# Splitting the remainder rows of a feed-forward's weights in two parts, and moving a set's sums on GpSimd

## The chip, the cores and the metric

The kernel runs on one core of one Trainium2 chip. The core has five engines that follow their own instruction lists and meet at semaphores: TensorE (PE, its weight loads PEld), VectorE (DVE), ScalarE (ACT), GpSimd (POOL) and SyncE (SP), which issues most of the DMAs. The metric is the device time of one execution in microseconds. Before the change it is 1981.64 us, the median of three runs (1973.98 to 1981.75).

## The reference

One transformer block on 2048 tokens of width 576, all in float32. The attention part (32 heads of 18, in four segments of 512 tokens with a memory) ends some 655 us into the execution and is not touched. What follows is the feed-forward part:

```
h = layernorm(x) * (1 + cb) + sb
x = x + gb * ((silu(h @ w_gate) * (h @ w_up)) @ w_down)
```

w_gate and w_up are 576 x 4608, w_down is 4608 x 576, and gb scales the 576 columns of the result.

## The kernel before

**Seven products in place of eight.** The kernel takes the product of h with a pair of 128-column blocks of w_gate (or w_up), cut in 2 x 2, with a Strassen-like scheme (Winograd's): seven products m = 1 to 7 of sums and differences of blocks. The seven weight operands of one set stand in the seven slots of a tile O. Slots 0, 1 and 2 (m = 1, 2, 4) come from memory as they are: the plain weights. Slots 4, 5, 3 and 6 (m = 5, 6, 7, 3) are sums that GpSimd makes of blocks in O, by `sum_o(p, z, j)` with j = 0 to 3 in that order (L1089).

**Two words per number.** TensorE reads float32 rounded to a shorter form, so each weight is split: `prep_w` casts a slot to wh on ScalarE (L1098), and VectorE subtracts wh from it to get wl (L1099). A product (`prod`, L1134) is seven matmuls of 512 columns. Six of them use wh and wl on 2 x 128 rows of the contraction. The seventh uses wr, the 32 remainder rows of the 288, which stand three times over in 96 partitions. The wr tile of a set holds all seven slots, 7 x 128 = 896 columns; `prep_r` casts it at once (L1083) and subtracts partitions 32 to 63 (L1084).

**Loops.** There are two halves, t = 0 and 1 of 1024 tokens, and in each 18 pairs p of column blocks. A pair has two sets, z = 0 (gate) and z = 1 (up), so 14 steps k, one product each: z = 0 in steps 0 to 6, z = 1 in 7 to 13, in the order m = 1, 3, 6, 2, 7, 5, 4. The product m = 3 is that of the other set, one set late: step 1 uses set 1 of the pair before, and step 8 uses set 0. In the first half steps 4 to 11 also multiply a chunk of the pair before by the down weights (`plain`, L1254, twelve matmuls of 288 columns into pd), and VectorE adds it to acc (L1258).

**Banks.** The products of a set add up in three PSUM banks, A, B and C, and partial results are copied out on the way. After m = 1 ScalarE copies A to B (the B copy, L1179). After m = 6 it copies A to tb, after m = 7 to tc (L1162). VectorE adds C and tb after m = 3 (in set 1 into cu, L1156) and C and tc after m = 5. The next product into a bank waits until what stands in it has been copied.

**What sets the order.** It is written out by hand: what a step emits stands in each engine's list in the order of the code, and each engine goes through its list in order. VectorE's subtractions are put in `later` and emitted at the start of the next step. `prep_w` runs five products ahead (PF = 5), in the order MP. For the first half, before the change:

- Step 1 loads the pair's down weights into RW (`load_d`, L1106, SP), once RW is free of the wd store of the pair before. GpSimd scales them by gb at steps 4 and 5 (`mul_d`, L1112) and makes their four differences for the second half at 6 to 9 (`sum_d`, L1117). `prep_d` splits the four plain blocks (L1123, L1124) at steps 5, 6, 7 and 10.
- Step 2 loads set 0 of the next pair into O (`load_o`, L1069, SP), step 9 loads set 1. O has two buffers, one per set, and a load waits until the last readers of the buffer are done.
- GpSimd makes set 0's sums at steps 6 to 8. Of set 1's it makes two at 10 and 11, the other two at 4 and 5 of the next pair, each in front of a `mul_d`.
- `prep_r` of set 1 stands at step 6, that of the next set 0 at 9 (at 8 ahead of the second half).
- ScalarE's queue stores to memory what the second half reads again: the sums (`store_o`, oD, L1075), the rows (`store_r`, rD, L1092) and the down weights (wd, L1436). The second half loads them in place of making them (L1072, L1080, L1108).
- From the second pair on, steps 2 to 11 each advance a generator by one (`prep2`, `next(g2)`). It prepares the second half's h in small pieces on all engines, with DMAs of its own on SP (xl and xh rows, xb, yD).

Of the kernel before, what the change touches and what calls it, by code (L numbers as in the profile page):

```python
# [8 lines left out]
F32R = mybir.dt.float32r  # L9
BF16 = mybir.dt.bfloat16  # L10
AF = mybir.ActivationFunctionType
ALU = mybir.AluOpType
# [3 lines left out]
P = 128  # L16
# [18 lines left out]
PF = 5  # L35
# [34 lines left out]
def f32(ap):  # L70
    return ap.bitcast(F32)
# [3 lines left out]
def block(ctx: ExitStack, tc: tile.TileContext, x, wqk, wv, wo, beta, wgu, wd, c, w_mod, out):  # L75
    nc = tc.nc
# [76 lines left out]
    rD = [[dr.tile([96, 7, P], F32, tag=f"rD{p}_{z}", name=f"rD{p}_{z}") for z in range(2)] for p in range(NF // 2)]  # L153
# [93 lines left out]
    with ExitStack() as p1:  # L247
# [78 lines left out]
        with ExitStack() as p0:  # L326
# [27 lines left out]
            for p in (1, 0):  # L354
                for k in range(6):
                    for h in range(2):
                        r = 64 * (1 - p) + 32 * h
# [534 lines left out]

    p4 = ExitStack()
    NPR = NF // 2
    MP = (1, 6, 2, 7, 5, 4, 3)
    ZM = [(z if m != 3 else 1 - z, m) for z in range(2) for m in (1, 3, 6, 2, 7, 5, 4)]
    SLOT = {1: 0, 2: 1, 3: 6, 4: 2, 5: 4, 6: 5, 7: 3}
    ACT_OP = {1: 0, 2: 1, 3: 2, 4: 6, 5: 3, 6: 4, 7: 5}
# [175 lines left out]
    def store_o(p, z):  # L1074
        nc.scalar.dma_start(oD[p][z], O[p, z][:, 3:7, 0:2])  # L1075

    def prep_r(t, p, z):
        R[z] = r = wrp.tile([P, 7, P], F32R, tag="wr", name="wr")
        if t == 1:
            nc.sync.dma_start(f32(r[0:96]), rD[p][z])  # L1080
            return
        o = O[p, z]
        nc.scalar.copy(r[0:96], o[0:96, :, 2, :])  # L1083
        later.append(lambda: nc.vector.tensor_tensor(r[32:64], o[32:64, :, 2, :], f32(r[32:64]), op=ALU.subtract))  # L1084

    def sum_o(p, z, j):
        o = O[p, z]
        d, a, b, op = ((4, 3, 2, ALU.add), (5, 4, 0, ALU.subtract), (3, 0, 3, ALU.subtract), (6, 1, 5, ALU.subtract))[j]
        nc.gpsimd.tensor_tensor(o[:, d], o[:, a], o[:, b], op=op)  # L1089
# [20 lines left out]
    def mul_d(p, f):  # L1110
        v = RW[p][:, 2 * f:2 * f + 2].rearrange("p a b -> p (a b)")
        nc.gpsimd.tensor_tensor(v, v, gbB, op=ALU.mult)  # L1112

    def sum_d(p, j):
        r = RW[p]
        d, a, b = ((4, 1, 0), (5, 3, 4), (6, 2, 5), (1, 3, 1))[j]
        nc.gpsimd.tensor_tensor(r[:, d], r[:, a], r[:, b], op=ALU.subtract)  # L1117
# [155 lines left out]
    with tc.manual_schedule():  # L1273
# [51 lines left out]
        for i in range(4):  # L1325
            for h in range(2):
                for c in range(WC):
                    n = 8 * i + 4 * h + c
                    wo_m(3, i, h, c, 2)
                    if n in TT:  # L1330
                        next(gt, None)
                    if c == 3:
                        wo_x(3, i, h)
                    if n in EE:
                        next(ge, None)
                    if n in SS:
                        j = SS.index(n)
                        sum_o(0, j // 4, j % 4)
                    if n == WW[0]:
                        prep_r(0, 0, 0)  # L1340
                    if n in WW:
                        prep_w(0, 0, next(gw))
                        flush()
                if h == 1 and i < 2:
                    wo_r(3, i + 2)
                    wo_s(3, i + 2)
                    wo_t(3, i + 2)
# [26 lines left out]
        for t in range(2):  # L1374
            for p in range(NPR):
                last = t == 1 and p == NPR - 1
                nx = (p + 1) % NPR
                tn = t if nx else t + 1
                if t == 0 and p == NPR - 1:
                    run(g2)  # L1380
                    p6.close()
                    accq = pool(p4, "acq")
                    new_acc(accq, (1, 6, 7))
                if last:
                    load_x11(1)
                chunk = 0
                for k in range(14):
                    z, m = ZM[k]
                    todo, later[:] = later[:], []
                    while nw < len(seq) and nw <= n + PF:  # L1390
                        prep_w(*seq[nw])
                        nw += 1
                    n += 1
                    for f in todo:
                        f()
                    if k != 1 or prev is not None:
                        step(z, m)
                    if k == 1 and prev is not None:
                        PA[0, 1] = AC[0, 1]
                    if t == 0 and p == NPR - 1 and k in (7, 9, 10, 11, 12, 13) or t == 1 and p == 0 and k == 1:  # L1400
                        load_y(ACT_OP[m])
                    swap = t == 1 and p == 0
                    if not last and k == 7 - PF + swap:
                        load_o(tn, nx, 0)
                    elif not last and k == 14 - PF:
                        load_o(tn, nx, 1)
                    if k == (2 if t else 6):
                        prep_r(t, p, 1)
                    elif not last and k == (8 if t == 0 and tn else 9):
                        prep_r(tn, nx, 0)  # L1410
                    if t == 0:
                        if k == 1:
                            load_d(0, p)
                        elif k == 4 or k == 5:
                            if p:
                                sum_o(p, 1, k - 2)
                            mul_d(p, k - 4)
                        elif 6 <= k < 10 and p < NPR - 2:
                            sum_d(p, k - 6)
                        if tn == 0:  # L1420
                            if 5 < k < 9:
                                sum_o(nx, 0, k - 6)
                            if k == 8:
                                sum_o(nx, 0, 3)
                            elif k in (10, 11):
                                sum_o(nx, 1, k - 10)
                        if k == 0 and p == 0:
                            store_o(p, 0)
                        elif k == 3:
                            store_r(p, 0)  # L1430
                        elif k == 7:
                            store_o(p, 1)
                        elif k == 9:
                            store_r(p, 1)
                        elif k == 11:
                            nc.scalar.dma_start(wdD[p][:, :NS[p]], RW[p][:, :NS[p]])  # L1436
                        elif k == 12 and tn == 0:
                            store_o(nx, 0)
                    elif k == 2 + 2 * swap:
                        load_d(1, p)  # L1440
                    if prev is not None and is_plain(*prev):
                        if k in (0, 2):
                            ij = (1, 0) if k == 0 else (0, 1)
                            prep_a(prev[1] % 2, ij, PA[ij])
                        if CH0[t][k]:
                            f = plain(*prev, chunk)
                            if f:
                                late[k + 3] = f
                            chunk += 1
                        due(k)  # L1450
                    elif prev is not None:
                        for j in range(4):
                            if k == KS[j]:
                                sum_a(j)
                        if k == 0:
                            prep_a(prev[1] % 2, 2, PA[1, 0])
                        for j, kk in KA:
                            if k == kk:
                                prep_a(prev[1] % 2, j, PA[ASRC[j]])
                        for _ in range(CH[k]):  # L1460
                            down(*prev, chunk)
                            chunk += 1
                    if last and 1 <= k < 9:
                        comb(k - 1)
                    if p == 0 and (t, k) in RS:
                        load_res(t, RS[t, k])
                    if is_plain(t, p):
                        if k in (5, 6, 7, 10):
                            j = (5, 6, 7, 10).index(k)
                            prep_d(p, (j // 2, j % 2), j)  # L1470
                    elif k >= 7:
                        prep_d(p, POS[k - 7], WSLOT[POS[k - 7]])
                    for ij, kk, j in (((0, 0), 11, 1), ((1, 1), 13, 4)):
                        if k == kk:
                            prep_a(p % 2, ij if is_plain(t, p) else j, AC[ij])
                    if t == 0 and k in G2 and p > 0:
                        next(g2, None)
                for k in sorted(late):
                    due(k)
                PA.clear()  # L1480
                PA.update(AC)
                prev = (t, p)
# [61 lines left out]
```

## Time and profile before

| | |
|---|---|
| median of the runs | 1981.64 us |
| the profiled execution's own time | 1983.39 us |
| its span, first to last instruction | 1981.7 us |
| mean granted TensorE clock | 0.986 |
| first half of the feed-forward | 658 to 1338 us |
| second half | 1338 us to the end |
| PE waiting for wr of L1084, 672 to 1333 us | 39.1 us, 18 times |
| GpSimd waiting for O's load, same stretch | 132.5 us, 17 times |

The page gives each engine's busy time. A matmul's end is modelled, and matmuls overlap, so idle time in front of a matmul counts from the modelled end of the one before. In the list of waits a line has who waited, for whom, the sum in us, how often, and the longest. In the timeline a line has the start, the duration, engine, line of the code, operation, output<-inputs, shape, and in brackets the idle time of the engine in front of it and what ended that. In a table of stretches a line has the stretch, its length, the busy time of PE, PEld, DVE, ACT and POOL with the instructions of each, the granted clock, the share of DMA time and GB/s. An engine's idle time only counts where the engine is the bound or holds it up.

### The profile page before, as it was taken

How to read it: one execution, taken by the hardware profiler on the slowest of the kernel's cores; microseconds unless marked ns; L12 is line 12 of the kernel's file. 1: busy time of each engine (PE TensorE's matmuls, PEld its weight loads, DVE VectorE, ACT ScalarE, POOL GpSimd, SP SyncE). 2: the span in 40 equal slices, each digit the busy share in tenths (PEclk: the TensorE clock that was granted, in tenths of full speed). 3: DMA queues.
4: the chain of work that ended last, by engine and by line, in shares of the span. 5: the costliest groups of instructions: out<-in, count | busy, mean ns of one | idle time of the engine just before them, and what ended most of it. 6: DMA issues, size and time to landing. Idle time of an engine off the chain costs nothing.

```text
span 1981.7 us, 30522 instructions
## 1 busy us (share of the span) xinstructions
PE 1893.4 (96%) x10927; PEld 1574.8 (79%) x10927; DVE 1500.3 (76%) x3231; ACT 924.9 (47%) x2000; POOL 580.3 (29%) x772
## 2 busy tenths in 40 slices
PE   7999989999998899999999999999999999999999
PEld 4888856676776677888888887888888888888888
DVE  6575258878786877777777777765888888888887
ACT  2222267767666533444444443443454544454442
POOL 5212235555535544444344444420000000000000
PEclk9999999999999899999999999999999999999999
DMA  7767564545435644444454454449433333232331
GB/s 220 234 225 248 208 189 121 144 134 152 133 109 146 198 151 146 159 155 149 159 171 145 143 161 133 137 145 312 151 98 113 104 97 117 85 113 95 119 102 67
DMA packets 173543, 296.63 MB, mean 150 GB/s; under 512 B 25104, under 2 KB 101776, under 8 KB 171920
## 3 DMA queue, kind: packets, MB, share of 16 engines
q1 hardware_dynamic: 143392, 237.43, 38.8%
q10 hardware_dynamic: 30000, 57.25, 8.1%
q8 instruction: 86, 1.41, 0.3%
q14 instruction: 65, 0.53, 0.1%
HBM read 185.29 MB, written 109.31 MB: 149 GB/s over the span
## 4 chain that ended last, share of the span: by engine, by line
PE 86%; DVE 6%; DMA 5%; issue 1%; ACT 1%; POOL 1%; SPq 1%; ACTq 0%; DVEq 0%; POOLq 0%
PE A L1134 21%; PE pd L1254 12%; PE C L1134 12%; PE pd L1237 9%; PE B L1134 6%; PE pp L101 4%; PE s L589 4%; PE av L609 4%; PE s L187 4%; PE pv L101 3%; PE pw L707 2%; DVE wr L1084 1%; DVE wl L1099 1%; DMA mD<-mr 1%; PE pn L778 1%
## 5 line engine op out<-in xcount | busy, mean ns | idle before, releaser
L1134 PE MATMUL A<-y,wh 128*128 128x512 f32 x1152 | 406.6, 393 | 1.8 <-ACT tb L1162 0.9
L192 DVE CUSTOM_DVE_ANT_0 junk<-s,tri 128x256 bf16<-128x256 f32 (+3 forms) x512 | 228.9, 487 | 77.9 <-PE s L187 70.3
L1099 DVE TENSOR_TENSOR wl<-O,wh 128x256 fp32r<-128x256 f32 x504 | 259.7, 518 | 3.0 <-ACT wh L1098 2.5
L1134 PEld LDWEIGHTS A<-y,wh 128*128 128x128 f32 x1152 | 217.3, 189 | 46.0 <-ACT tb L1162 1.7
L1089 POOL TENSOR_TENSOR O<-O 128x384 f32<-128x384 f32 x144 | 166.5, 1165 | 229.0 <-DMA O<-in_wgu_dram 132.5
L1258 DVE TENSOR_TENSOR acc<-acc,pd 128x576 f32<-128x576 f32 x156 | 117.4, 753 | 151.4 <-PE pd L1254 151.3
L592 ACT ACTIVATE Pt<-s 128x512 f32<-128x512 f32 (+1 forms) x352 | 186.6, 558 | 88.5 <-PE s L589 73.7
L1134 PE MATMUL A<-y,wl 128*128 128x512 f32 x576 | 227.1, 394 | 0.0
L1134 PE MATMUL C<-y,wh 128*128 128x512 f32 x576 | 206.5, 399 | 0.0
L1242 DVE TENSOR_TENSOR acc<-acc,pd 128x576 f32<-128x576 f32 x216 | 162.1, 751 | 55.5 <-PE pd L1237 48.0
L1098 ACT CAST wh<-O 128x256 fp32r<-128x256 f32 x504 | 197.6, 404 | 0.1
L1254 PE MATMUL pd<-dh,al 128*128 128x288 f32 x640 | 192.5, 301 | 0.0
L1254 PE MATMUL pd<-dh,ah 128*128 128x288 f32 x640 | 192.2, 300 | 0.0
L1254 PE MATMUL pd<-dl,ah 128*128 128x288 f32 x640 | 192.0, 300 | 0.0
L589 PE MATMUL s<-qs,ks 110*128 110x512 f32 (+2 forms) x384 | 151.3, 411 | 5.5 <-DMA qs<-mD 3.9
L1198 DVE TENSOR_TENSOR al<-sg,ah 128x512 fp32r<-128x512 f32 x192 | 146.3, 762 | 13.6 <-ACT ah L1197 13.4
L1197 ACT CAST ah<-sg 128x512 fp32r<-128x512 f32 x192 | 118.6, 618 | 79.7 <-DVE sg L1157 79.5
L1134 PE MATMUL A<-y,wr 96*128 96x512 f32 x288 | 117.2, 407 | 40.4 <-DVE wr L1084 39.1
L187 PE MATMUL s<-ks,qs 108*128 108x256 f32 (+3 forms) x512 | 142.3, 329 | 3.0 <-DMA ks<-kD 1.2
L1149 ACT ACTIVATE sg<-sg 128x512 f32<-128x512 f32 x73 | 46.2, 633 | 196.6 <-DVE sg L1148 196.6
L1237 PE MATMUL pd<-dh,ah 128*128 128x288 f32 x448 | 133.0, 297 | 0.0
L1237 PE MATMUL pd<-dh,al 128*128 128x288 f32 x448 | 132.5, 296 | 0.0
(349 smaller groups left out, 4470.8 us busy)
## 6 DMA issues: line engine op xcount, KB each, us to landing
O<-in_wgu_dram SPq DMA_DIRECT2D x36, 768.0 KB
oD<-O ACTq DMA_DIRECT2D x36, 512.0 KB
O<-oD SPq DMA_DIRECT2D x36, 512.0 KB
ks<-kD SPq DMA_DIRECT2D x68, 216.0 KB
qs<-qD SPq DMA_DIRECT2D x68, 216.0 KB
O<-in_wgu_dram SPq DMA_DIRECT2D x36, 384.0 KB
rD<-wr ACTq DMA_DIRECT2D x36, 336.0 KB
wr<-rD SPq DMA_DIRECT2D x36, 336.0 KB
```

The costliest lines, as they stand in the source:

```text
L187: nc.tensor.matmul(bank[:, n * (h - h0):n * (h - h0) + n], lhsT=qst[b][0:108, h, 128 * i:128 * i + 128], rhs=kst[b][0:108, h // 2, 0:n], s ...
L192: nc.vector.tensor_tensor_reduce(junk[:, :n], bank[:, n * (h - h0):n * (h - h0) + n], tri[:, L - n:], 1.0, -3e38, op0=ALU.add, op1=ALU.max ...
L589: nc.tensor.matmul(bank[:, n * (g - h):n * (g - h + w)].rearrange("p (a b) -> p a b", a=w), lhsT=kst[u % NB][0:110, g // 2, 128 * j:128 * ...
L592: nc.scalar.activation(pt[:, h:h + per, :n], bank[:, :n * per].rearrange("p (a b) -> p a b", a=per), AF.Exp, scale=SCALE)
L1089: nc.gpsimd.tensor_tensor(o[:, d], o[:, a], o[:, b], op=op)
L1098: nc.scalar.copy(wh, o)
L1099: later.append(lambda: nc.vector.tensor_tensor(wl, o, f32(wh), op=ALU.subtract))
L1134: nc.tensor.matmul(bank, lhsT=a, rhs=b, start=(first and n == 0), stop=(n == 6), skip_group_check=not first)
L1198: later.append(lambda: nc.vector.tensor_tensor(al, src, f32(ah), op=ALU.subtract))
L1237: nc.tensor.matmul(pd[:, i, :288], lhsT=a[:, tk], rhs=w, start=(k == 0), stop=(k == 2))
L1242: nc.vector.tensor_tensor(o, o, pd[:, :, :288], op=ALU.add)
L1254: nc.tensor.matmul(pd[:, i, :288], lhsT=a[:, tk], rhs=w, start=(k == 0), stop=(k == 5))
```

## The change

- `prep_r` takes a part: part 0 is slots 0 to 2 (the plain weights, 384 columns), part 1 slots 3 to 6 (the sums, 512 columns), each with its own cast and subtraction. In the first half set 1's parts stand at steps 3 and 7, the next set 0's at 9 and 10.
- All four of set 1's sums move to steps 2 to 4 of the pair that uses them, in front of `mul_d`, which moves to 5 and 6. Set 0's sums move to 7 to 9, the differences of the down weights to 6, 7, 9 and 10.
- In the first half set 1 is loaded at step 12 in place of 9.
- m = 2 is split ahead of m = 6 (MP), and the casts of the down weights move to 6, 7, 8 and 10.
- The stores move: oD of set 1 from step 7 to 6, rD of set 1 from 9 to 10, wd from 11 to 12, oD of the next set 0 from 12 to 13.
- The second half's first load of set 1's rows goes to ScalarE's queue, at step 3 in place of 2.

```diff
-    MP = (1, 6, 2, 7, 5, 4, 3)
+    MP = (1, 2, 6, 7, 5, 4, 3)
...
-    def prep_r(t, p, z):
-        R[z] = r = wrp.tile([P, 7, P], F32R, tag="wr", name="wr")
+    def prep_r(t, p, z, part=0):
+        if part == 0:
+            R[z] = wrp.tile([P, 7, P], F32R, tag="wr", name="wr")
+        r = R[z]
         if t == 1:
-            nc.sync.dma_start(f32(r[0:96]), rD[p][z])
+            (nc.sync if p or z == 0 else nc.scalar).dma_start(f32(r[0:96]), rD[p][z])
             return
-        o = O[p, z]
-        nc.scalar.copy(r[0:96], o[0:96, :, 2, :])
-        later.append(lambda: nc.vector.tensor_tensor(r[32:64], o[32:64, :, 2, :], f32(r[32:64]), op=ALU.subtract))
+        o, c = O[p, z], slice(0, 3) if part == 0 else slice(3, 7)
+        nc.scalar.copy(r[0:96, c], o[0:96, c, 2, :])
+        later.append(lambda: nc.vector.tensor_tensor(r[32:64, c], o[32:64, c, 2, :], f32(r[32:64, c]), op=ALU.subtract))
...
                         prep_r(0, 0, 0)
+                        prep_r(0, 0, 0, 1)
...
-                    elif not last and k == 14 - PF:
+                    elif not last and k == (14 - PF if tn else 12):
                         load_o(tn, nx, 1)
-                    if k == (2 if t else 6):
-                        prep_r(t, p, 1)
-                    elif not last and k == (8 if t == 0 and tn else 9):
-                        prep_r(tn, nx, 0)
-                    if t == 0:
+                    if t:
+                        if k == 2 + swap:
+                            prep_r(1, p, 1)
+                        elif not last and k == 9:
+                            prep_r(1, nx, 0)
+                    else:
+                        if k in (3, 7):
+                            prep_r(0, p, 1, k // 7)
+                        elif tn == 0 and k in (9, 10):
+                            prep_r(0, nx, 0, k - 9)
+                        elif tn and k == 8:
+                            prep_r(1, 0, 0)
                         if k == 1:
                             load_d(0, p)
-                        elif k == 4 or k == 5:
-                            if p:
-                                sum_o(p, 1, k - 2)
-                            mul_d(p, k - 4)
-                        elif 6 <= k < 10 and p < NPR - 2:
-                            sum_d(p, k - 6)
-                        if tn == 0:
-                            if 5 < k < 9:
-                                sum_o(nx, 0, k - 6)
-                            if k == 8:
-                                sum_o(nx, 0, 3)
-                            elif k in (10, 11):
-                                sum_o(nx, 1, k - 10)
+                        elif k in (2, 3, 4) and p:
+                            for j in ((0, 1), (2,), (3,))[k - 2]:
+                                sum_o(p, 1, j)
+                        elif k in (5, 6):
+                            mul_d(p, k - 5)
+                        if tn == 0 and k in (7, 8, 9):
+                            for j in ((0,), (1, 2), (3,))[k - 7]:
+                                sum_o(nx, 0, j)
+                        if k in (6, 7, 9, 10) and p < NPR - 2:
+                            sum_d(p, (6, 7, 9, 10).index(k))
...
-                        elif k == 7:
+                        elif k == 6:
                             store_o(p, 1)
-                        elif k == 9:
+                        elif k == 10:
                             store_r(p, 1)
-                        elif k == 11:
+                        elif k == 12:
                             nc.scalar.dma_start(wdD[p][:, :NS[p]], RW[p][:, :NS[p]])
-                        elif k == 12 and tn == 0:
+                        elif k == 13 and tn == 0:
                             store_o(nx, 0)
-                    elif k == 2 + 2 * swap:
+                    if t and k == 2 + 2 * swap:
                         load_d(1, p)
...
-                        if k in (5, 6, 7, 10):
-                            j = (5, 6, 7, 10).index(k)
+                        if k in (6, 7, 8, 10):
+                            j = (6, 7, 8, 10).index(k)
                             prep_d(p, (j // 2, j % 2), j)
```

## The prediction, made before the result was known

> **What bounds the kernel now.** I read the page first (engine shares, then the slices), then the stretches of the two halves, the waits inside the first half, and the timeline around the largest of them.
>
> ```profile
> span 1981.7 us, 30522 instructions
> PE 1893.4 (96%) x10927; PEld 1574.8 (79%) x10927; DVE 1500.3 (76%) x3231; ACT 924.9 (47%) x2000; POOL 580.3 (29%) x772
> ...
> 658.00:1338.00 680.00, 638.22 (x3387) 555.12 (x3386) 517.09 (x765) 295.89 (x656) 295.28 (x265) 0.98 0.48 156
> 1338.00:1982.00 644.00, 638.15 (x3459) 559.60 (x3457) 532.12 (x970) 290.50 (x676) 0.00 (x0) 1.00 0.38 121
> ```
>
> TensorE is the bound. The last two lines are the two halves of the feed-forward (length, then busy time of PE, PEld, DVE, ACT and POOL, the granted clock, DMA). The second half leaves PE 5.9 us unbusy, the first, which the change edits, 41.8, and there the clock is 0.98 and not 1.00. What PE lacks stands in the waits between 672 and 1333 us:
>
> ```profile
> PEld A L1134 <- DVE wr L1084: 46.8, 18, 3.6
> PE A L1134 <- DVE wr L1084: 39.1, 18, 3.2
> ...
> ACT tb L1162 <- DVE cu L1156: 20.3, 10, 3.0
> ```
>
> One wait per pair, 18 in all, for the subtraction that ends the rows' split. The timeline shows why (start, duration, engine; in brackets the idle time in front):
>
> ```profile
> 899.75 0.93 ACT L1083 CAST wr<-O 96x896 fp32r<-96x896 f32 x1
> ...
> 900.86 0.75 DVE L1258 TENSOR_TENSOR acc<-acc,pd 128x576 f32<-128x576 f32 x1 [0.74 <-PE pd L1254]
> ...
> 901.53 0.52 DVE L1099 TENSOR_TENSOR wl<-O,wh 128x256 fp32r<-128x256 f32 x1
> ...
> 902.09 1.76 DVE L1084 TENSOR_TENSOR wr<-O,wr 32x896 fp32r<-32x896 f32 x1
> ...
> 903.91 0.51 PE L1134 MATMUL A<-y,wr 96*128 96x512 f32 x1 [1.70 <-DVE wr L1084]
> ```
>
> The rows are cast at step 6 and subtracted at the start of step 7. On VectorE the subtraction stands behind the accumulation of step 6's chunk, which can't begin before PE ends that chunk. From there VectorE needs 0.75 + 0.52 + 1.76 = 3.0 us, while PE has only six matmuls, 1.4 us, before step 7's seventh asks for the rows.
>
> **What the wait is worth.** The row's 39.1 us count from the modelled end of a matmul (0.39 us after its start), while starts that nothing holds are 0.23 apart: 0.16 more each, so 39.1 + 18 x 0.16 = 42.0 us. Some waits also cost clock. After the one at 744.79 (2.93 us) the matmuls stand 0.43 apart, and the 288-wide ones 0.24 and not 0.13:
>
> ```profile
> 747.42 0.63 PE L1134 MATMUL C<-y,wh 128*128 128x512 f32 x1
> 747.85 0.63 PE L1134 MATMUL C<-y,wl 128*128 128x512 f32 x1
> ```
>
> Six at +0.11 and four at +0.20 make 1.5 us. Of stretches cut one to a pair, seven or eight show such a clock (0.95 to 0.97): 7.5 x 1.5 = 11 us; bounds 0 and, from the mean clock of 0.98 over 666 us, 13.3.
>
> **The change part by part.** Steps are numbered as in the loop: 0 to 3, 12 and 13 take PE 1.62 us each, 4 to 11, with a chunk, 3.2.
>
> Rows in two parts. Set 1's plain part (384 of 896 columns) is cast at step 3 and subtracted at 4, three steps before its use at 7; the sums' part is cast at 7, subtracted at 8, used at 9. For that one the distance from the end of step 7's chunk to the use is 1.62 + 1.6 + 1.4 = 4.6 us, and VectorE needs 0.75 (accumulate) + 1.65 (the slow wl at 965.82, beside GpSimd) + 1.1 for 512 columns slowed as the 896 above (1.76 for 1.08) = 3.5. The wait goes: -42.0 and -11; what is late next, the sums' part, has 1.1 us of cover. Set 0's parts (steps 9, 10) precede uses at 0 and 2 by three steps or more.
>
> More instructions: 37 more casts and subtractions. From 256 columns at 0.42 and 896 at 1.08 a subtraction has a fixed 0.16, 6 us on VectorE in all; a cast (0.40, 0.93) a fixed 0.19, 7 us on ScalarE. They hide in VectorE's 128.4 us of waiting for pd (110 times) and ScalarE's idle half: 0, bound +6.
>
> Set 1's sums. Before, two stood at steps 10 and 11, where GpSimd waited for the load (132.5 us in 17 waits, off the path), and two among the multiplications. Now all four run as soon as the load lands, ahead of mul_d, and so fall near steps 12 to 4, where VectorE is densest. That stretch now, in the pair from 959.95 on:
>
> ```profile
> 962.48 1.43 POOL L1112 TENSOR_TENSOR dr__11702<-dr__11702,gbB 128x576 f32<-128x576 f32 x1 [4.89 <-DMA dr__11702<-in_wd_dram]
> ...
> 962.91 1.56 DVE L1198 TENSOR_TENSOR al<-sg,ah 128x512 fp32r<-128x512 f32 x1 [0.75 <-ACT ah L1197]
> ...
> 964.39 0.68 DVE L1156 TENSOR_TENSOR cu<-C,tb 128x512 f32<-128x512 f32 x1
> ...
> 965.17 0.59 ACT L1162 COPY tb<-A 128x512 f32<-128x512 f32 x1 [1.69 <-DVE cu L1156]
> ...
> 966.41 0.40 PE L1134 MATMUL A<-y,wh 128*128 128x512 f32 x1
> ```
>
> An al of 0.68 alone takes 1.56 beside GpSimd; cu frees tb; tb is copied out of bank A until 965.76; step 4 writes that bank at 966.41: 0.65 us of margin. In ten pairs this copy waits for VectorE already. I put the margin at 0.5. Four sums (mean 1165 ns) can each hold one VectorE operation: half a sum each is 2.3 us, less the 0.9 that the multiplication costs there today, 1.4; less the margin, 0.9 per pair. Where the load lands early (sums over before step 12) or late (after cu), nothing. I take half of 17 pairs: +8; bounds 0 and 17 x 3.2 = +54 (all four held in full, 4.6, less 0.9 and 0.5).
>
> By the Trainium skill (SBUF — State Buffer, section on its two separate sides) VectorE with two SBUF inputs and GpSimd share a port pair under an exclusive lock, and the later one waits for the whole instruction. The trace agrees: GpSimd's 1.43 from 962.48 plus 0.68 ends at 964.59, the al ended at 964.47. By that rule every sum in this stretch blocks, which is rival B.
>
> Set 1's load, moved on the SyncE queue from step 9 to 12. A load now takes 5.0 us (issued 910.87, first sum 915.88). It waits no longer for a buffer, but the second half's DMAs of steps 9 to 11 stand ahead of it, and where one belongs to step 11 it issues some 1.5 us into step 12, 958.3 on this scale. It lands at 963.3, or 966.3 with 3 us for the 1008 KB wd store, which now issues beside it. ScalarE casts wh from it at step 2, in front of the tb copy, so it must land by 965.4. About six pairs have such a DMA: 0 to 6 x 0.9; I take +3. In the others it lands earlier. Behind it in the queue, load_d waits for the wd store anyway, one step later than now.
>
> mul_d, with the sums in front: loaded up to 3 us later, then 4.7 of sums, then 1.4: about 13 us into the pair. The casts that need it move to step 6, 12.9 us in, behind ScalarE's other work there: 0, cover about 1 us. What queues behind a late one is the B copy of step 7.
>
> Set 0's sums for the next pair move from steps 6 to 8 to 7 to 9 and sum_d's spread to 10; the first cast that reads them is at 11 and the wd store at 12, more than 3 us off: 0. Swapped weights order: set 1's m=6 is cast at step 4 (used at 9), m=2 at 3 (used at 10): still five steps ahead, 0. Stores one step later, oD of set 1 one earlier: issues of 0.3 to 0.5 us on ScalarE's queue, 0. Second half's first rows on ScalarE's queue: PE's one wait for rD is 1.3 us; -1.3, at worst 0.
>
> Sum against the profiled execution's 1983.39: 1983.4 - 42.0 - 11 + 8 + 3 - 1.3 = 1940.1. That execution stood 1.75 above the median of the runs: **1938**.
>
> **Rivals.** A, the sum above: 1938, on its own 1925 (no new cost, clock bound 13.3) to 1950.
> B, the sums hold VectorE in every pair: 2.3 less a margin of 0.4 is 1.9 x 17 = 32 us in place of 8 and 3: about 1960. For it: ten waits on cu, al's 1.56. Against: GpSimd's multiplication and sums stand from 2.5 us into the pair already, and PE waited for tb there once, 0.9 us.
> C, slower: the load lands too late. From 5.5 us into the pair on, each us of delay holds wh, behind it the tb copy, and PE at step 4, one for one. The 54 us of gain are spent at 3.2 us over 17 pairs, a landing 8.7 us in. Landing at 11 costs 5.5 x 17 = 94 and, with long waits, the clock: some 2020. For it: GpSimd waits up to 14.4 us for such loads. Against: those waits count from where GpSimd was ready; issue to landing is 5 us, DMA share 0.48.
> D, the change doesn't remove the wait: it goes to the sums' part at step 9. 1.1 us of slack speak against it; about 1980.
>
> **Chances.** A 0.58, B 0.26, D 0.06, C 0.10. Half a per cent, 10 us, is about what a measurement of this kernel can tell from no change. A and B are faster by more (0.84), D the same (0.06), C slower (0.10). The range, 1925 to 1966, runs from A's best bound to a little beyond B.
>
> **What would show it.** Right: no PE or PEld wait on wr in the first half; its clock near 1.00; its stretch about 637 us long (680 less 43); new waits of PE for tb of some 8 us; GpSimd's waits for O shorter. For B: PE waits for tb or B in nearly every pair, wl and al longer on the mean than 518 and 762 ns. For C: ScalarE's wh waiting for DMA O<-in_wgu_dram. Wrong outright: a first half as long as before though the wait on wr is gone.

## The result, and the profile after

The changed kernel takes 1950.18 us in the median of four runs (1944.18 to 1955.34), against 1981.7 of the kernel before beside it (four runs, 1973.98 to 1984.54): a ratio of 0.9846, with a 95% interval of 0.9805 to 0.9887. Measured once more, in a later comparison, it took 1941.45 (1939.77 to 1955.54) against 1983.2: 0.9814 (0.9766 to 0.9862). It is faster, by 1.5 to 1.9%. Its eight executions fall into shorter ones (1940 to 1948 us) and longer ones (1952 to 1956 us, at a mean clock of 0.988 to 0.989 where the shorter have 0.991 to 0.995); none of the longer ones was profiled, so what costs them is open. Forecast were 1938 us and a range of 1925 to 1966.

The profiled execution took 1944.18 us. First the top of its page:

```profile
span 1942.5 us, 30570 instructions
...
PE 1884.8 (97%) x10927; PEld 1568.8 (81%) x10927; DVE 1522.1 (78%) x3267; ACT 925.9 (48%) x2036; POOL 581.8 (30%) x772
```

And the two halves as stretches (length, busy time of PE, PEld, DVE, ACT and POOL, granted clock, share of DMA time, GB/s):

```profile
658.00:1309.00 651.00, 637.69 (x3447) 556.50 (x3446) 545.81 (x815) 299.05 (x697) 296.69 (x265) 0.99 0.51 168
1309.00:1943.00 634.00, 627.92 (x3404) 550.92 (x3403) 526.25 (x960) 288.14 (x670) 0.00 (x0) 1.00 0.37 117
```

The second half's first product starts at 1309.0 us. In the kernel before it starts at 1348.0; the 1338 of the table before and of the prediction was set 10 us too early. The same cut of the kernel before reads:

```profile
658.00:1348.00 690.00, 648.22 (x3441) 563.93 (x3440) 523.31 (x777) 298.35 (x662) 295.28 (x265) 0.98 0.49 158
1348.00:1982.00 634.00, 628.15 (x3404) 550.79 (x3402) 525.90 (x960) 288.04 (x670) 0.00 (x0) 1.00 0.37 117
```

PE's unbusy time in the two halves comes out the same by this cut (41.8 and 5.9 us), so no step of the prediction hangs on it. The second half lasts 634 us both times. All of the gain is in the first half, 690 to 651, where PE's unbusy time falls from 41.8 to 13.3.

The waits of the first half (660 to 1309 us; who waited, for whom, sum in us, times, longest). These are all of PE's and PEld's of 0.7 us or more:

```profile
PEld A L1136 <- ACT tb L1164: 11.0, 8, 2.8
PE A L1136 <- ACT tb L1164: 7.8, 6, 2.4
PEld pd L1256 <- DVE acc L1260: 6.0, 4, 3.8
PE pd L1256 <- DVE acc L1260: 4.1, 2, 3.4
PEld A L1136 <- ACT cu L1164: 1.2, 1, 1.2
PEld A L1136 <- ACT B L1181: 1.1, 3, 0.4
PEld pt L1036 <- DVE acc L1260: 0.7, 1, 0.7
PE A L1136 <- ACT cu L1164: 0.7, 1, 0.7
```

No line names wr any more. In its place stand two others: the wait for tb in step 4, forecast, and one for acc, which was not.

**Where the time went.** I compared each distance between the starts of two matmuls with the usual distance of that pair of tiles (the shortest fifth), over the first half. What is more than 0.25 us over counts as a wait, the rest as a slower pace, which is where a lower clock shows.

| us in the first half | before | after |
|---|---|---|
| its length, first product to first product of the second half | 689.5 | 649.1 |
| waits in front of wr's matmul | 42.1 (18) | 0 |
| waits in front of a product's first matmul (tb, cu, B) | 1.9 (2) | 9.7 (7) |
| waits in front of the chunk's matmuls (acc) | 0.9 (3) | 4.7 (3) |
| other waits | 1.5 | 0.7 |
| slower pace | 24.7 | 16.0 |

The columns add up to 71.1 and 31.1, and the difference of 40.0 is nearly all of the 40.4 by which the half got shorter.

**The pair with the largest wait for tb**, which starts at 937.00. The timeline has start, duration, engine, line, operation, shape, and idle time in brackets:

```profile
934.00 5.04 POOL L1091 TENSOR_TENSOR O<-O 128x384 f32<-128x384 f32 x4 [7.72 <-DVE dl L1126]
...
939.55 3.01 POOL L1114 TENSOR_TENSOR dr__11734<-dr__11734,gbB 128x576 f32<-128x576 f32 x2 [0.52 <-DMA dr__11734<-in_wd_dram]
...
939.84 1.42 DVE L1101 TENSOR_TENSOR wl<-O,wh 128x256 fp32r<-128x256 f32 x1
...
941.18 1.92 DVE L1200 TENSOR_TENSOR al<-sg,ah 128x512 fp32r<-128x512 f32 x1
942.51 1.25 POOL L1119 TENSOR_TENSOR dr__11734<-dr__11734 128x288 f32<-128x288 f32 x1
943.03 1.02 DVE L1101 TENSOR_TENSOR wl<-O,wh 128x256 fp32r<-128x256 f32 x1
943.97 0.68 DVE L1200 TENSOR_TENSOR al<-sg,ah 128x512 fp32r<-128x512 f32 x1
944.57 0.68 DVE L1158 TENSOR_TENSOR cu<-C,tb 128x512 f32<-128x512 f32 x1
...
945.36 0.58 ACT L1164 COPY tb<-A 128x512 f32<-128x512 f32 x1 [4.18 <-DVE cu L1158]
...
946.00 0.50 PE L1136 MATMUL A<-y,wh 128*128 128x512 f32 x1 [2.38 <-ACT tb L1164]
```

The load came early here, the four sums were over at 939.04, and so mul_d and the first difference of the down weights ran without a pause from 939.55 to 943.76. In that time VectorE's operations take 1.42, 1.92 and 1.02 us, where the same forms take 0.42 and 0.68 alone. cu starts 7.6 us into the pair. With GpSimd idle between step 12 and cu it starts at 3.56 (six of the 17 pairs from the second on). Up to about 5.0 that costs nothing: here step 4 begins 1.43 us after cu, and where nothing holds it, it begins 6.45 us into the pair.

This goes through all pairs: the more GpSimd time lies between the start of step 12 and cu, the later cu starts. In the changed kernel 0 us of it go with 3.56, 0.5 with 3.9, 1.4 with 3.8 to 4.3, 4.8 to 5.3 with 5.3 to 6.5, and 8.9 to 9.3 with 7.6.

### The profile page after: what moved, and what is told of

The parts are those of the page before. It is cut to its first block, busy times and chain, and to the rows that moved or that the text cites. A ratio compares the mean times of both kernels' runs of the same rounds, so it can differ in the third digit from the quotient of the medians.

```text
span 1942.5 us, 30570 instructions
## 1 busy us (share of the span) xinstructions
PE 1884.8 (97%) x10927; PEld 1568.8 (81%) x10927; DVE 1522.1 (78%) x3267; ACT 925.9 (48%) x2036; POOL 581.8 (30%) x772
## 4 chain that ended last, share of the span: by engine, by line
PE 84%; DVE 7%; DMA 5%; issue 1%; ACT 1%; POOL 1%; SPq 0%; ACTq 0%; DVEq 0%; POOLq 0%
PE A L1136 22%; PE pd L1256 13%; PE C L1136 10%; PE pd L1239 9%; PE B L1136 5%; PE pp L101 5%; PE s L589 4%; PE av L609 4%; PE s L187 4%; PE pv L101 3%; PE pw L707 2%; DVE wl L1101 1%; DMA mD<-mr 1%; DVE al L1200 1%; DVE y L938 1%
## 5 line engine op out<-in xcount | busy, mean ns | idle before, releaser
L1136 PE MATMUL A<-y,wh 128*128 128x512 f32 x1152 | 408.6, 395 | 10.1 <-ACT tb L1164 7.8
L1101 DVE TENSOR_TENSOR wl<-O,wh 128x256 fp32r<-128x256 f32 x504 | 271.4, 540 | 5.4 <-ACT wh L1100 4.8
L1100 ACT CAST wh<-O 128x256 fp32r<-128x256 f32 x504 | 198.5, 404 | 11.5 <-DMA O<-in_wgu_dram 10.8
L1136 PE MATMUL C<-y,wh 128*128 128x512 f32 x576 | 202.5, 392 | 0.0
L1256 PE MATMUL pd<-dl,ah 128*128 128x288 f32 x640 | 189.6, 296 | 0.0
L1200 DVE TENSOR_TENSOR al<-sg,ah 128x512 fp32r<-128x512 f32 x192 | 152.1, 792 | 12.1 <-ACT ah L1199 11.6
L1239 PE MATMUL pd<-dl,ah 128*128 128x288 f32 x448 | 132.3, 295 | 0.0
```

What stands on the lines that cost most here:

```text
L1100: nc.scalar.copy(wh, o)
L1101: later.append(lambda: nc.vector.tensor_tensor(wl, o, f32(wh), op=ALU.subtract))
L1136: nc.tensor.matmul(bank, lhsT=a, rhs=b, start=(first and n == 0), stop=(n == 6), skip_group_check=not first)
L1200: later.append(lambda: nc.vector.tensor_tensor(al, src, f32(ah), op=ALU.subtract))
L1239: nc.tensor.matmul(pd[:, i, :288], lhsT=a[:, tk], rhs=w, start=(k == 0), stop=(k == 2))
L1256: nc.tensor.matmul(pd[:, i, :288], lhsT=a[:, tk], rhs=w, start=(k == 0), stop=(k == 5))
```

## The experiments

Theory G: the wait for wr is gone with the split alone, and what is left to gain in the first half is VectorE held by GpSimd between step 12 and cu. The rivals: the moves of the sums and of the load have a share in the gain; or the late load (prediction's C) is what the changed kernel still loses; or the longer sums, wherever they are, cost in proportion. A diff is against the kernel that the text names.

**One part at a time.** The split of the rows alone, on the kernel before (`prep_r` gets its parts as in the change):

```diff
...
-                    if k == (2 if t else 6):
-                        prep_r(t, p, 1)
-                    elif not last and k == (8 if t == 0 and tn else 9):
-                        prep_r(tn, nx, 0)
+                    if t:
...
+                    elif k in (3, 7):
+                        prep_r(0, p, 1, k // 7)
+                    elif tn == 0 and k in (9, 10):
+                        prep_r(0, nx, 0, k - 9)
...
```

> The kernel before with only the rows split in two (set 1 at steps 3 and 7, the next set 0 at 9 and 10); sums, loads, stores, multiplications and the order of the weights stay. Theory A (the split alone ends PE's wait, and the moves only add waits: in the changed kernel PE and PEld wait 7.8 and 11.0 us for tb): PE's waits for wr in the first half are gone, waits for tb stay at 1 to 3 us, and the time is 8 to 15 us below the changed kernel, 1935 to 1942. Theory R (the moves carry part of the gain, since without them GpSimd sits waiting for the load at steps 10 and 11 and holds up what queues behind it): the time is 5 us or more above the changed kernel, over 1955.

Measured: 1945.54 us (1945.28 to 1946.17), ratio 0.9823 (0.9793 to 0.9853). PE now waits for wr in one place alone, 0.7 us. And all the moves alone, the rows whole (all seven slots in one cast), on the changed kernel:

```diff
...
-                        if k in (3, 7):
-                            prep_r(0, p, 1, k // 7)
-                        elif tn == 0 and k in (9, 10):
-                            prep_r(0, nx, 0, k - 9)
+                        if k == 6:
+                            prep_r(0, p, 1)
+                        elif tn == 0 and k == 10:
+                            prep_r(0, nx, 0)
```

> The changed kernel with the rows whole again: one cast of 896 columns at step 6 for set 1, at step 10 for the next set 0; everything else as changed. Theory A: PE waits for wr as before (about 39 us in 18 waits, the slow clock with it) and for tb as in the changed kernel: 1981 + 8 to 12, 1985 to 1995. Theory R: 1970 or less.

Measured: 1989.76 us (1986.69 to 1996.33), ratio 1.0055 (1.0035 to 1.0076). Its waits, 660 to 1300 us, hold both kinds:

```profile
PEld A L1136 <- DVE wr L1086: 43.6, 16, 6.0
PE A L1136 <- DVE wr L1086: 36.7, 16, 5.6
...
PE A L1136 <- ACT tb L1164: 7.9, 7, 2.4
```

The split makes the gain. The moves without it are slower by about half a per cent; with it they are worth nothing that the runs can tell (1945.54 against 1950.18 and 1941.45). And the wait for tb is not brought by the moves alone: with the split alone it is there too, though I had expected 1 to 3 us of it there and a time of 1935 to 1942.

```profile
PEld A L1136 <- ACT tb L1164: 14.4, 9, 2.9
...
PE A L1136 <- ACT tb L1164: 10.6, 9, 2.4
```

**The wait removed in another way.** The kernel before, set 1's rows whole, but cast at step 5, with its last two sums both at step 4:

```diff
-                    if k == (2 if t else 6):
+                    if k == (2 if t else 5):
...
-                            if p:
-                                sum_o(p, 1, k - 2)
+                            if p and k == 4:
+                                sum_o(p, 1, 2)
+                                sum_o(p, 1, 3)
```

> The kernel before with the rows of set 1 whole, cast at step 5 in place of 6, and for this both remaining sums of set 1 at step 4 in front of the first multiplication. If what matters is the distance between VectorE's subtraction and its use and not the split, PE's wait for wr goes here as well: from the end of step 5's chunk to the use are 4.6 us, VectorE needs 0.75 + 1.65 + 1.76 = 4.2 at worst; 1935 to 1945. If the split is needed (the whole subtraction too long, or ScalarE held at step 5 by GpSimd's late sums), waits for wr or for the B copy of 10 us or more stay: 1950 to 1975.

Measured: 1952.34 us (1949.94 to 1955.53), ratio 0.9858 (0.9826 to 0.989). PE waits 0.8 us for wr, in two places, and 14.7 for tb:

```profile
PE A L1134 <- ACT tb L1162: 14.7, 9, 2.4
PE A L1134 <- DVE wr L1084: 0.8, 2, 0.5
```

So for the wait for wr it is the distance between the subtraction and its use that counts, not the size of the parts. The time is above the 1935 to 1945 that I had expected, and 7 us above the split alone; the longer wait for tb (14.7 for 10.6) is part of that, the rest is open.

**The load's place.** The changed kernel with set 1's load back at step 9:

```diff
-                    elif not last and k == (14 - PF if tn else 12):
+                    elif not last and k == 14 - PF:
```

> The changed kernel with set 1's load of the first half back at step 9. Theory A with the late load as the cost: ScalarE's waits of 10.8 us for the load in front of wh go and the time falls by 3 to 5 us. Theory A with the sums' contention as the cost: now the sums run early in every pair, as in the pairs at 937 and 976, where PE waited 2.5 and 2.4 us for tb; the time rises by 10 to 30 us.

Measured: 1945.27 us (1942.34 to 1947.4), ratio 0.982 (0.9783 to 0.9857). ScalarE's waits for the load are gone and so is PE's wait for acc, but the wait for tb is longer (12.2 us, 10 times): the sums are earlier and leave mul_d in front of cu in more pairs. The time can't be told from the changed kernel's (1950.18 and 1941.45), so the late load's cost and its worth about cancel.

**More sums.** The changed kernel beside an unchanged copy of itself (1941.45 us, the second measurement above), with three of set 1's four sums made twice:

```diff
-                            for j in ((0, 1), (2,), (3,))[k - 2]:
+                            for j in ((0, 0, 1, 1), (2,), (3, 3))[k - 2]:
```

> The changed kernel once more, beside the others on one chip. Its first four runs spread from 1944 to 1955 us, those of the split alone from 1945.3 to 1946.2. If the moves are worth nothing, 1944 to 1955 again with a median within 5 us of the split alone.

> The changed kernel with three of set 1's four sums made twice (the same result, 3.5 us more of GpSimd in front of the multiplications in each pair). Theory G (what is left of PE's loss is GpSimd's time between step 12 and cu in step 1: in four traces cu starts 3.6 us into the pair where GpSimd worked under 1.5 us there, near 5.4 at 5 us and 7.6 at 8 to 9): the pairs whose load lands before cu get up to 3.5 us more of it, PE's waits for tb rise from 8 to 25 to 45 us, 1965 to 1990. Rival L (the late landing, in front of wh on ScalarE, is the cost): ScalarE's waits for the load stay at 10 us and the time within 8 us of the changed kernel.

Measured: 1941.89 us (1941.65 to 1942.38), ratio 0.9794 (0.9769 to 0.9818): no cost that the runs can tell, and theory G as I had put it missed. Where set 1's sums begin ahead of cu, GpSimd was busy up to cu already, with sums and then mul_d. The added sums mostly push mul_d behind cu, and GpSimd's time between step 12 and cu stays within 0.7 us of what it was in 14 of the 17 pairs (in one it falls by 1.2 us, in two it rises by 1.8 and 3.1). G had to be put in terms of that time, not of the number of sums.

**A steady landing.** The changed kernel with set 1 loaded from ScalarE's queue at step 12:

```diff
-            nc.sync.dma_start(o[:, 0:4], wgu[p, z])
+            (nc.scalar if p and z else nc.sync).dma_start(o[:, 0:4], wgu[p, z])
```

> The changed kernel with set 1's load of the first half issued from ScalarE's queue at step 12, where it can't run ahead, in place of SyncE's, which issues it anywhere from step 9 on. Theory G: the sums start after cu or shortly before it in every pair, as in the pairs of the changed kernel where cu starts at 3.56 us; GpSimd's time between step 12 and cu falls under 2 us, PE's waits for tb to 0 to 4 us, 1930 to 1938. Rival L: now every pair has a late load, ScalarE's waits for it in front of wh go from 10.8 us to 25 or more and hold the tb copy: 1950 to 1965.

Measured: 1944.02 us (1942.28 to 1945.73), ratio 0.9804 (0.9779 to 0.983). The place that I expected was wrong: the load did not land behind cu but in front of it, so that the sums start 0.6 to 1.0 us into 16 of 17 pairs. That is the condition of the prediction's rival B, made true. GpSimd has 4.2 to 7.0 us between step 12 and cu in these pairs, cu starts at 5.2 to 7.5, and 12.2 us of waits stand in front of the products' first matmuls, 14 in all, 0.87 each.

The same with the load one step later, at 13:

```diff
-                    elif not last and k == (14 - PF if tn else 12):
+                    elif not last and k == (14 - PF if tn else 13):
```

> The changed kernel with the first half's load of set 1 issued by ScalarE at step 13, behind its store of wd, in place of SyncE at step 12. Theory G (what is left on the path in the first half is VectorE held by GpSimd between step 12 and cu in step 1): the load lands 3.5 to 4.5 us into the pair, the sums start behind cu, GpSimd's time between step 12 and cu falls to 0 to 1.5 us, cu starts 3.6 to 4.3 us into the pair, PE waits for tb in at most 4 pairs, 1930 to 1940 us. Rival (rival C of the prediction: a late landing holds ScalarE's wh and behind it the tb copy): ScalarE waits for the load in most pairs, PE waits for tb as often as before or more, 1948 to 1965.

Measured: 1936.82 us (1935.83 to 1939.28), ratio 0.9789 (0.976 to 0.9817). Now the sums start 2.5 to 4.6 us into 16 of the 17 pairs and reach at most one sum in front of cu: 0 to 1.6 us of GpSimd time there, cu at 3.56 to 4.3. The last pair has 5.4 us and cu at 7.0, and there PE waits for tb, 1.9 us:

```profile
PEld pd L1256 <- DVE acc L1260: 5.2, 7, 2.2
PEld A L1136 <- ACT tb L1164: 4.1, 2, 2.3
PE A L1136 <- ACT tb L1164: 3.3, 2, 1.9
ACT wh L1100 <- DMA O<-in_wgu_dram: 3.1, 3, 1.2
PE pd L1256 <- DVE acc L1260: 2.8, 2, 1.8
```

With nothing but the load, and so the sums, one step later the median falls by 7.2 us (1944.02 to 1936.82). The two kernels were measured at different times, and the intervals of their ratios overlap. But the traces say the same: the first half is 8.0 us shorter (648.2 to 640.3), and the waits in front of the products' first matmuls fall from 12.2 to 4.5 us. That is what G says, and ScalarE's waits for the load, 3.1 us for 10.8 in the changed kernel, speak against rival C.

**VectorE's other work.** The subtraction of set 1's al stands at step 0, in front of cu. On the kernel with only the rows split I moved it to step 1, behind cu:

```diff
-                        if k in (0, 2):
-                            ij = (1, 0) if k == 0 else (0, 1)
+                        if k in (1, 2):
+                            ij = (1, 0) if k == 1 else (0, 1)
```

> The split alone with one more move: the cast and subtraction of the (1, 0) activations go from step 0 to step 1, so that this al (0.68 us alone, up to 1.9 beside GpSimd) stands behind cu on VectorE and not in front. Theory G with VectorE's own order: cu comes 0.7 to 1.9 us earlier in the pairs that are late, PE's waits for tb fall from 10.6 to 2 to 5 us, 1936 to 1941. Rival: GpSimd holds whatever stands next, a wl in place of the al, and the chunk at step 4 then waits for al: 1944 to 1950.

Measured: 1935.28 us (1934.32 to 1936.04), ratio 0.976 (0.9735 to 0.9785), the fastest kernel of the study: 10.3 us less than with the split alone (0.9823), in another comparison. With one operation fewer to be held, cu starts at 3.43 in eight of the 17 pairs, and PE waits 5.0 us for tb in place of 10.6:

```profile
PE A L1136 <- ACT tb L1164: 5.0, 4, 1.8
```

The traced first half is 10.1 us shorter (650.9 to 640.7). By the table's columns 5.9 us of that are waits in front of the products' first matmuls and 4.4 the slower pace. The same edit on the changed kernel with its load at step 9:

> The changed kernel with set 1 loaded at step 9 as before the change, and al of set 1 behind cu. The same edit on the kernel with only the rows split took 10 us. Theory G: VectorE has one operation less between step 12 and cu, each of which GpSimd can hold; cu starts 0.7 to 1.5 us earlier in the pairs where GpSimd works there, PE waits for tb in about half as many pairs, 1933 to 1940 us. If the moves of the sums have a cost of their own elsewhere, it stays at 1941 to 1948.

Measured: 1937.55 us (1936.6 to 1938.44), ratio 0.9789 (0.9755 to 0.9822), 7.7 us less than 1945.27. The intervals of the two ratios overlap, but the traced first half is 9.2 us shorter (653.7 to 644.5). And on the kernel with the load at step 13:

> The run before, and the subtraction of set 1's al moved from step 0 to step 1, behind cu. If al in front of cu is what remains of VectorE's queue there, no wait of PE for tb stays and it is 2 to 5 us faster than the run before, 1928 to 1937. If the load comes too late (rival C), moving al changes nothing, 1948 to 1965. If GpSimd's sums behind cu now hold al and the wl of step 2 instead, PE waits for wl or al take the place of those for tb, and the two are equal.

Measured: 1944.1 us (1943.08 to 1945.03), ratio 0.9823 (0.9795 to 0.9851). It is 7.3 us slower than without the move, though cu now starts at 3.43 in 15 of the 17 pairs. The third of the expected cases came true, and it cost where I had expected a draw:

```profile
PEld pd L1256 <- DVE acc L1260: 11.7, 10, 5.1
PE pd L1256 <- DVE acc L1260: 7.6, 7, 4.6
PEld pd L1256 <- DVE al L1200: 4.4, 2, 3.2
PE pd L1256 <- DVE al L1200: 3.9, 2, 2.9
```

GpSimd's work is now behind cu, but for at most 1.0 us of it, in every pair but the last, and al was put right beside it. VectorE is held just the same, two or three steps later, and what comes late then is acc and al, for which the chunk's matmuls wait. The largest, 4.63 us in front of the chunk at 1170.62, in the timeline of this kernel:

```profile
1165.90 3.88 DVE L1086 TENSOR_TENSOR wr<-O,wr 32x384 fp32r<-32x384 f32 x1
1166.48 2.89 POOL L1091 TENSOR_TENSOR O<-O 128x384 f32<-128x384 f32 x3
...
1169.81 0.75 DVE L1260 TENSOR_TENSOR acc<-acc,pd 128x576 f32<-128x576 f32 x1
...
1170.62 0.40 PE L1256 MATMUL pd<-dh,ah 128*128 128x288 f32 x1 [4.63 <-DVE acc L1260]
```

The subtraction of wr, 0.55 us when nothing is beside it, takes 3.88 beside three sums, and the accumulation stands behind it. So theory G is shown for the wait for tb by the load's place and by al's, though that time alone does not set cu (with the load at step 9 one pair has 2.7 us of it and cu at 5.9). And it is a special case: VectorE is held wherever the two engines meet, and what that costs depends on what stands behind it on VectorE at that moment.

## Why the prediction was right, point by point

**The wait for wr, -42.0 and the clock, -11.** The first is right to 0.1 us: 42.1 in front of 18 matmuls before, none after. What is late next, the sums' part at step 9, had its slack, and rival D is out. The slower pace fell by 24.7 - 16.0 = 8.7 us, inside the bounds of 0 and 13.3 and 2.3 below the value taken. Behind two of the new waits the clock is low as well: 0.50 from 985.80 to 989.20 and from 1252.00 to 1255.40.

**Sums that hold VectorE, +8, and the late load, +3.** Together 11, measured 9.7 - 1.9 = 7.8. The sizes are near, the reasons right only in part, so the nearness is partly luck. The step said that a load that lands early costs nothing, since the sums are over before step 12. In no pair are they over that early. The two pairs that lose most, 2.4 to 2.5 us each, have the earliest loads: their sums start 3.0 and 4.3 us ahead of the pair and are over 2.0 and 1.3 us into it, in time for cu, but mul_d follows, 2.5 and 2.9 us into the pair, and holds VectorE in their place. The step costed the sums and forgot what comes forward behind them on GpSimd. I had charged these waits to the moves. But the kernel before has 1.9 us of them, the split alone 14.1, the moves alone, with the wait for wr still there, 10.4, and both together 9.7: either edit brings them. That the old wait had given VectorE and GpSimd time to catch up would explain what the split brings, but no run shows it apart. The late load was where I had put it, in six pairs:

```profile
ACT wh L1100 <- DMA O<-in_wgu_dram: 10.8, 6, 3.0
```

Of these only two held PE, 0.7 and 0.1 us: most of ScalarE's delay lay in its own slack.

**The second half's rows, -1.3.** Not gained. The rows are there in time, but at the start of the second half PE then waits for y, loaded from SyncE's queue, 1.5 us, once.

**The steps that failed** are those that costed the added casts and subtractions, and mul_d behind the sums, at nothing, with VectorE's and ScalarE's idle time as the cover. The wait for acc (4.7 us, 0.9 before) is not in the sum at all. Most of it is one place, where a subtraction of 0.42 us took 6.54:

```profile
1241.24 6.54 DVE L999 TENSOR_TENSOR st<-t,st 32x256 fp32r<-32x256 f32 x1
1241.77 1.98 POOL L1091 TENSOR_TENSOR O<-O 128x384 f32<-128x384 f32 x2
...
1243.72 2.81 POOL L1114 TENSOR_TENSOR dr__14861<-dr__14861,gbB 128x576 f32<-128x576 f32 x2
...
1246.49 3.28 POOL L1091 TENSOR_TENSOR O<-O 128x384 f32<-128x384 f32 x3
1247.81 1.10 DVE L1101 TENSOR_TENSOR wl<-O,wh 128x256 fp32r<-128x256 f32 x1
1248.95 1.23 DVE L1086 TENSOR_TENSOR wr<-O,wr 32x384 fp32r<-32x384 f32 x1
1250.21 0.75 DVE L1260 TENSOR_TENSOR acc<-acc,pd 128x576 f32<-128x576 f32 x1
...
1251.02 0.40 PE L1256 MATMUL pd<-dh,ah 128*128 128x288 f32 x1 [3.38 <-DVE acc L1260]
```

The sum on the terms as measured: -42.1 - 8.7 + 7.8 + 3.8 - 0.8 = -40.0. With the first half starting 1.4 us later (659.9 for 658.5) and the rest 0.2 shorter the profiled execution is 39.2 us faster, 1983.39 to 1944.18; forecast were 43.3. Against the forecast median of 1938 the two measured ones lie 12.2 and 3.5 us higher.

**The rivals.** B needed waits in nearly every pair; there are six or seven. Its other sign, longer means of wl and al, came true all the same (columns: count, busy time and mean in ns, idle time before):

```profile
L1101 DVE TENSOR_TENSOR wl<-O,wh 128x256 fp32r<-128x256 f32 x504 | 271.4, 540 | 5.4 <-ACT wh L1100 4.8
...
L1200 DVE TENSOR_TENSOR al<-sg,ah 128x512 fp32r<-128x512 f32 x192 | 152.1, 792 | 12.1 <-ACT ah L1199 11.6
```

540 and 792 ns for 518 and 762: 22 x 504 + 30 x 192 ns are 17 us of VectorE's time. By the stretches all of it is in the first half, where VectorE's busy time goes from 523 to 546 us (the added subtractions are in it); in the second, without GpSimd, it stays at 526. B's price was tried in the run with the load on ScalarE's queue at step 12: 0.87 us a wait, as the 0.9 per pair of the prediction, and not B's 1.9. C's mechanism shows in two pairs of the changed kernel: the wh cast that waited for the load begins 6.2 and 5.6 us into the pair, and PE is held by 0.7 and 0.1 us, what lies beyond C's 5.5. But C needed this in every pair, and some 3 us of it.

## What to carry to other kernels

When a wait in the middle of a loop is taken away, look for the waits behind it: here a quarter of what went (11.6 of 50.8 us) came back as waits that hardly showed before. Count a second engine's work by where its whole run of queued instructions lies against the first engine's urgent ones, not by the one instruction that is moved; a change of about 2 us in one load's landing, or of one subtraction by one step, moved the traced first half by 8 to 10 us, down in three kernels and up in one. The smaller edit, the split and al behind cu, beat the larger one by 6 us where both were measured together (1935.28 and 1941.45).

## What was unexpected about the hardware

A VectorE operation can be held by several GpSimd instructions in a row. In the changed kernel a subtraction of 0.42 us took 6.54, though the cast that it reads had ended 1.1 us before it began, while GpSimd ran six instructions without a pause (1240.62 to 1247.50), and ended 0.28 us after the last of them. With the load at step 13 a wl of 0.41 us took 5.69, with al moved as well one took 5.63, and both ended 0.28 us after GpSimd's last instruction, the fifth in a row. In the kernel before the longest wl takes 2.22, held through three instructions. The Trainium skill (SBUF — State Buffer, section on its two separate sides) has the later of the two blocked for the whole instruction of the earlier. Most places here agree, such as the al of 1.92 us above beside instructions of 1.5: of the 173 VectorE subtractions, additions and products in the changed kernel's first half that took over 0.15 us longer than the shortest of their form, 169 were held by no GpSimd instruction that started after them. These do not agree, since up to five GpSimd instructions that started later went ahead of the waiting one. A pause of GpSimd is not needed to let VectorE in: the wr of 3.88 us above ended 0.41 us after the end of a sum, with the next instruction already running. Why VectorE gets its turn after one instruction in most places and after three to six in others is not settled by these runs.

The length of a wait does not decide alone whether TensorE's clock falls behind it. In the kernel before the granted clock went to 0.50 for 3.4 us (once for 6.8) with eight of the 18 waits for wr, as the prediction's seven or eight. Behind one of 2.0 us it fell (0.50 from 1097.40 to 1100.80), behind one of 3.1 us it did not (1.00 from 784.90 to 788.30). In the changed kernel it fell behind the wait for tb that ended at 984.90 (2.4 us) and not behind the one that ended at 946.00 (2.5 us). What decides it is not tested here.
